# Attention and a gated MLP on one core: blocks of four slots as two or three visits with a written order, and tanh behind the scores

## The chip, the cores and the metric

One core of one Trainium2 chip. The time is that of one execution of the program on the device, in microseconds; all times below are in microseconds unless marked otherwise. The kernel before took 1624.26 in the median of three runs (1623.45 to 1624.9).

## The reference

The input x is 2048 tokens by 512 features. It is normalised (layernorm without gain), then goes through two branches: attention with 32 heads of 16 features, and an MLP of 512 to 1792 to 512 with a squared ReLU. The attention output is multiplied by silu of the MLP output and added to x.

```python
qkv = x @ wqkv                                     # 32 heads of 16
scores = einsum("bhqd,bhkd->bhqk", q, k) * 16 ** -0.5
s = softmax(scores) @ v  ->  @ wo
h = xn @ w1 + b1; r = where(h > 0, h, 0); out = (r * r) @ w2 + b2
return x + s * silu(out)
```

All of it is float32. The kernel keeps that precision by splitting operands into a high and a low part and running three matmuls for each product; attention scores carry the parts in extra rows of 64-row operands.

## The kernel before

**Slots and units.** Attention is cut into 32 units (a group of four heads and 512 queries), and each unit into 16 slots of 128 keys: 512 slots in all. A slot st has four **scores** (`exp_mm`, matmul on line 1225: 64 rows, 512 columns; then an exponential on ACT, line 1231, into a tile `pt` or `ex`) and, two slots later, one **PV** step (`pv_mm`, line 382): four column tiles of 128 rows by 32 columns, accumulated in the bank `po`. At the end of a unit `evac` copies `po` on ACT and starts a chain that divides by the row sums.

**Maxima.** The softmax needs the maximum of each row before the unit's first score. It is made ahead by `max_mm` (line 306: the same product once more; then a reduce on DVE, line 314): 64 maxima for each unit, 2048 in all. When a unit's maxima are complete, `max_end` notes it, and `shift_due` calls `shift` (lines 337 to 359): four short DVE instructions, and DMAs on SP that write the result into rows of the unit's query tiles.

**Dense work.** The MLP and the output product are run in between by a generator, `dense`. From slot 60 on most of it comes in blocks of four slots: 12 dense units (D) for each of the two **row tiles** of TensorE (partitions 0 to 63 and 64 to 127, the *lanes* 0 and 1). A D is one matmul of 512 columns (second MLP product and output product) or two of 256 (`first_pair`, first MLP product), on line 240 or 790. The two lanes add into one PSUM bank `pd_t`; the second lane's first matmul is made to wait for an instruction (`last_use`) that shows that the first lane is done. At the end of the block `post` empties the bank on ACT (two ReLUs, or a copy). Between the blocks stand stretches of four plain slots (`slot`, line 1356) with six D each.

**Banks.** Scores go through three PSUM banks (`se`), maxima through three others (`pm_t`), `pd_t` and `po` have one each. So the fourth score waits for the first one's exponential, and the fourth maximum for the first one's reduce.

**Who sets the order.** PE, ACT, DVE, POOL and SP run in the order in which the Python code records their instructions; no scheduler moves them. `long_slots` (line 1405) writes the order of a block: two halves h, each with the D of lane h. A half is either one **visit** of 14 steps per lane (all 12 D and two scores on lane h; six scores and seven maxima on the other) and then two PV steps in one group, or a visit of ten steps and one of four, each with one PV step behind it; that has eight maxima. `seven(st)` chooses the double form where the maxima are far enough ahead (`ahead_m`), always for two halves in a row: the second of a block and the first of the next. `visit` writes a column of the two strings at a time: the other lane's instruction, then its own.

**The gate.** After the second MLP product of 128 tokens, `gate` (line 579) is run three slots later, by `begin` at the start of a slot: tanh on ACT (line 581), two POOL instructions, and a DMA to `g_d`, which the output blocks read much later.

Of the kernel before, what the change touches and what calls it, by code (L numbers as in the profile page):

```python
# [18 lines left out]
D = 512  # L19
# [9 lines left out]
NCK = S // CW  # L29
# [4 lines left out]
EVAC = (1, 5, 6, 8, 12, 15)  # L34
EVAC_LAST = (1, 4, 5, 6, 8, 10)
EPS = 1e-5
LEAD_AT = (
    (3, 8, 12, 17, 22, 26, 31, 36, 40, 45, 48),
    (1, 6, 12, 15, 20, 24, 29, 33, 38, 42, 47),
# [4 lines left out]
def kernel(  # L44
# [54 lines left out]
    with ExitStack() as ph:  # L99
# [268 lines left out]
                    waiting.append((16 * u - 9, back))  # L368

        in_loop = []  # L370

        def shift_rows(u, p, i):
                    nc.sync.dma_start(
# [69 lines left out]
        def mlp_tasks(mp):  # L443
# [119 lines left out]
            def second(c, tt):  # L563
                hT = state["hT"]
                ps = pd.tile([P, D], F32, name="pd_t")
                u = up.tile([P, D], F32, name="u")
                th = rs[tt].rearrange("p a b -> p (a b)")
                ts_ = slice(tt * P, (tt + 1) * P)

                if c == 0 and tt == 0:  # L570
                    for k in range(5, FO):
                        later(k - 4, lambda k=k: load_w2(k, 2))

                def post():
                    nc.scalar.activation(u, ps, AF.Copy)  # L575
                    nc.gpsimd.tensor_tensor(u, u, b2_t, op=ALU.add)  # L576
                    later(3, gate)

                def gate():

                    nc.scalar.activation(th, u, AF.Tanh, scale=0.5)
                    nc.gpsimd.tensor_scalar(th, th, 0.5, 0.5, op0=ALU.mult, op1=ALU.add)
                    nc.gpsimd.tensor_tensor(u, u, th, op=ALU.mult)
                    t0 = c * CW + tt * P
                    later(4, lambda: nc.sync.dma_start(g_d[t0 : t0 + P, :], u))

                mms = terms3(ps, [
                    (lambda a, q, fo=fo: hT[q, a, fo, ts_], lambda b, q, fo=fo: w2t[q, b, fo])
                    for fo in range(FO)
                ])  # L590
                if c == 0:
                    yield from halves(mms, (6,) * 7, post, 1)
                    return
                if c == NCK - 1 and tt:

                    for i, task in enumerate(halves(mms, (6,) * 7, post, 1)):
                        if i == 4:
                            gone_pt.extend(rot["ex"])
                            free_pt[:] = [t for t in free_pt if all(t is not x for x in gone_pt)]
                        yield task  # L600
                    return

                if tt:
                    yield from halves(mms[:6], (6,), None, 1)
                    mms = mms[6:]
                for k in range(0, 36, 12):
# [626 lines left out]
        pts = {}  # L1233
# [95 lines left out]
        pos = {}  # L1329

        def pv_step(st, pts):
            u, kb = divmod(st, 16)
            if kb == 0:
                pos[0] = pv.tile([P, 512], F32, name="po")
            pv_mm(pos[0], u // 4, kb, pts)
            free_pt.extend(t for _, t in sorted(pts.items()) if all(t is not x for x in gone_pt))
            if kb == NT - 1:
                if u < NU - 2:
                    evac(pos[0], u)
                elif u == NU - 2:  # L1340
                    unit_inner(pos[0])
                else:
                    unit_final(pos[0])
# [61 lines left out]
        def long_slots(st0, units, post, wide=False):  # L1405
# [5 lines left out]
            def s(lane):  # L1411
                kb, j = todo[lane].pop(0)
                return exp_mm(kb, j, pts[kb], False)

            def visit(h, mine, theirs, h_first=False):
                own, other, follow = units[h], 1 - h, True
                for i, ops in enumerate(zip(mine, theirs)):
                    for lane in (h, other) if h_first else (other, h):
                        o = ops[0] if lane == h else ops[1]
                        if o == "D":  # L1420
                            own.pop(0)()
                        elif o == "m":
# [8 lines left out]
            wrap = [post] if post is not None else []  # L1431
            for h in range(2):
                st = st0 + 2 * h
                if st > st0:
                    begin(st)
                n = len(units[h])
                if wide:
                    for i, o in enumerate("sDsDDsDDDs"):
                        for lane in range(2):
                            if o == "s":  # L1440
                                s(lane)
                            else:
                                units[lane].pop(0)()
                    if wrap and not units[0]:
                        wrap.pop()()
                    begin(st + 1)
                    shift_due()
                    for kb in (st - 2, st - 1):
                        pv_step(kb, pts.pop(kb))
                elif n == 12 and seven(st):  # L1450
                    visit(h, "s" + "D" * n + "s", ".mmsmssmsmssmm")
# [122 lines left out]
```

## Time and profile before

| | before |
|---|---|
| median of three runs | 1624.26 (1623.45 to 1624.9) |
| the profiled execution | 1623.24 |
| its span, first to last instruction | 1621.4 |
| mean granted TensorE clock | 0.999 |
| PE busy | 1607.4 (99% of the span) |
| DVE busy | 1339.5 (83%) |
| ACT busy | 1184.9 (73%) |
| POOL busy | 526.4 (32%) |
| DMA traffic | 201.43 MB, mean 124 GB/s |

The page first gives each engine's busy time, then the chain of work that ended last, then groups of equal instructions with their number, the mean duration of one and the idle time ahead of them. Rows of the timeline begin with the start in us from the span's start and the duration of the row; a row with x7 merges seven instructions. In rows of PEld (weight loads) and the other engines, what stands in brackets is the idle time before and what ended it. `64*128` is a matmul on 64 rows and 128 columns of the array, `128*32` one on 128 rows and 32 columns. A row of the windows gives, for a stretch, its length, then busy time and number of instructions of PE, PEld, DVE, ACT and POOL, the granted clock, the DMA share and GB/s.

### The profile page before, as it was taken

The page shows a single profiled execution, that of the slowest core. Times are in us where ns is not written, and L with a number is a line of the kernel's source. Part 1 is how long each engine was busy: PE and PEld are TensorE (multiplying, and loading weights), DVE is VectorE, ACT ScalarE, POOL GpSimd, SP SyncE. Part 2 cuts the span into 40 slices and gives each one's busy share as a digit, 9 for nine tenths or more (in the row PEclk, how much of TensorE's full clock was granted, in tenths as well). Part 3 has the DMA queues.
Part 4 walks back from the last instruction along what each step waited for, and adds up shares of the span by engine and source line. Part 5 has one row for each costly group of instructions (what it writes and reads, how often), then busy time and mean ns, then how long its engine had stood idle before and what let it go on. Part 6 is the DMA issues. An engine that isn't in the chain of part 4 may idle for free.

```text
span 1621.4 us, 35371 instructions
## 1 busy us (share of the span) xinstructions
PE 1607.4 (99%) x13639; PEld 963.5 (59%) x13639; DVE 1339.5 (83%) x2327; ACT 1184.9 (73%) x2345; POOL 526.4 (32%) x549
## 2 busy tenths in 40 slices
PE   8999999999999999999999999999999999999998
PEld 6888665556556655665566556645665565554455
DVE  6499888888887888888888888888888888888833
ACT  6311777778777877777777778877877777777785
POOL 6635568223213320331132113311331133213334
PEclk9999999999999999999999999999999999999999
DMA  8895645334233631442342513333432342416443
GB/s 300 236 291 183 217 143 173 112 91 139 60 92 96 152 96 57 118 124 60 84 131 88 126 55 118 104 98 80 134 102 65 104 133 65 104 50 171 124 156 137
DMA packets 150464, 201.43 MB, mean 124 GB/s; under 512 B 50008, under 2 KB 67416, under 8 KB 148760
## 3 DMA queue, kind: packets, MB, share of 16 engines
q1 hardware_dynamic: 150296, 199.17, 41.9%
q8 instruction: 108, 1.77, 0.5%
q14 instruction: 60, 0.49, 0.1%
HBM read 144.84 MB, written 53.99 MB: 123 GB/s over the span
## 4 chain that ended last, share of the span: by engine, by line
PE 99%; DVE 0%; DMA 0%; ACT 0%; issue 0%; SPq 0%; DVEq 0%; ACTq 0%
PE po L382 31%; PE pd_t L240 18%; PE pm_t L306 17%; PE se L1225 15%; PE pd_t L208 6%; PE se L988 3%; PE se L1027 3%; PE pd_t L790 2%; PE po L1027 1%; PE pd_t L1027 1%; PE pm_t L1086 0%; PE pm_t L1225 0%; DMA xt<-in_A_x_dram 0%; PE pm_t L824 0%; PE se L872 0%; DVE mx L314 0%
## 5 line engine op out<-in xcount | busy, mean ns | idle before, releaser
L314 DVE TENSOR_REDUCE mx<-pm_t 128x1 f32<-128x512 f32 x2048 | 1266.2, 683 | 205.0 <-PE pm_t L306 111.9
L1231 ACT ACTIVATE pt<-se 128x512 f32<-128x512 f32 x1731 | 923.3, 613 | 217.9 <-PE se L1225 157.0
L306 PE MATMUL pm_t<-ka,qm 64*128 64x512 f32 x2048 | 790.0, 416 | 0.9 <-DVE mx L314 0.6
L1225 PE MATMUL se<-qe,ka 64*128 64x512 f32 x2009 | 728.4, 411 | 0.0
L382 PE MATMUL po<-pt,v 128*32 128x512 f32 x3540 | 527.9, 603 | 0.0
L306 PEld LDWEIGHTS pm_t<-ka,qm 64*128 64x128 f32 x2048 | 359.6, 184 | 219.8 <-DVE mx L314 199.5
L1225 PEld LDWEIGHTS se<-qe,ka 64*128 64x128 f32 x2009 | 349.8, 184 | 92.4 <-ACT pt L1231 63.9
L240 PEld LDWEIGHTS pd_t<-xc,w1s 64*128 64x128 f32 x2352 | 295.2, 187 | 53.0 <-issue 51.1
L240 PE MATMUL pd_t<-xc,w1s 64*128 64x256 f32 x2352 | 323.2, 286 | 0.0
L240 PE MATMUL pd_t<-w2t,hT 64*128 64x512 f32 x936 | 253.0, 406 | 0.0
L382 PE MATMUL po<-ex,v 128*32 128x512 f32 x556 | 233.9, 603 | 0.0
L1231 ACT ACTIVATE ex<-se 128x512 f32<-128x512 f32 x278 | 166.7, 614 | 49.9 <-PE se L1225 33.3
L240 PEld LDWEIGHTS pd_t<-w2t,hT 64*128 64x128 f32 x936 | 160.0, 184 | 50.5 <-issue 41.1
L382 PEld LDWEIGHTS po<-pt,v 128*32 128x32 f32 x3540 | 87.4, 108 | 150.1 <-issue 136.5
L557 POOL TENSOR_TENSOR r<-r 128x512 f32<-128x512 f32 x49 | 51.0, 1041 | 322.3 <-ACT r L554 322.3
L576 POOL TENSOR_TENSOR u<-u,b_t 128x512 f32<-128x512 f32 x16 | 20.6, 1289 | 361.3 <-ACT u L575 334.7
L208 PE MATMUL pd_t<-w2t,hT 64*128 64x512 f32 x408 | 106.0, 392 | 0.0
L208 PEld LDWEIGHTS pd_t<-w2t,hT 64*128 64x128 f32 x408 | 72.5, 184 | 10.3 <-DVE mx L314 0.7
L420 POOL TENSOR_TENSOR ot<-ot,hl 128x512 f32<-128x512 f32 x31 | 39.9, 1287 | 117.0 <-DMA hl<-r_d 86.7
L790 PE MATMUL pd_t<-wot,oc 64*128 64x512 f32 x267 | 76.1, 404 | 0.0
L84 POOL TENSOR_TENSOR hT<-r,hT 128x512 fp32r<-128x512 f32 x56 | 72.4, 1292 | 4.7
L554 ACT ACTIVATE r<-pd_t,b_t 128x256 f32<-128x256 f32 x98 | 42.2, 496 | 28.7 <-PE pd_t L240 28.7
(137 smaller groups left out, 1204.2 us busy)
## 6 DMA issues: line engine op xcount, KB each, us to landing
w1s<-w_d SPq DMA_DIRECT2D x196, 256.0 KB
xn_d<-xT SPq DMA_DIRECT2D x8, 1024.0 KB
qm<-q_d SPq DMA_DIRECT2D x128, 64.0 KB
qe<-q_d SPq DMA_DIRECT2D x128, 64.0 KB
ka<-k_d SPq DMA_DIRECT2D x32, 256.0 KB
hl<-r_d SPq DMA_DIRECT2D x31, 256.0 KB
k_d<-hl SPq DMA_DIRECT2D x30, 256.0 KB
q_d<-hl SPq DMA_DIRECT2D x15, 512.0 KB
```

Source lines behind the costliest of these rows:

```text
L84: (lo or nc.gpsimd).tensor_tensor(dst[1], raw, dst[0].bitcast(F32), op=ALU.subtract)
L208: mm = nc.tensor.matmul(out_, lh(r), rh(r), start=first_ and lane == 0, stop=last_ and lane == 1, skip_group_check=True,)
L240: mm = nc.tensor.matmul(out_, lh(r), rh(r), start=first_ and lane == 0, stop=last_ and lane == 1, skip_group_check=True,)
L306: nc.tensor.matmul(ps, qms[u][p][64 * j : 64 * j + 64, qb * P : (qb + 1) * P], kas[qd, p][64 * j : 64 * j + 64, kc * 512 : (kc + 1) * 512] ...
L314: return nc.vector.tensor_reduce(mxs[u][:, c, kc : kc + 1], ps, axis=AX.X, op=ALU.max)
L382: nc.tensor.matmul(po[32 * j : 32 * j + 32, :], vs[qd][:, (4 * kb + j) * VW : (4 * kb + j) * VW + 32], pts[j], start=(kb == 0), stop=(kb = ...
L557: nc.gpsimd.tensor_tensor(r, r, r, op=ALU.mult)
L790: inst = nc.tensor.matmul(ps[lane], oc[r, a, n, ts_], wot[r, b, n], start=m == 0 and (lane == 0 or wide), stop=m == kos and (lane == 1 or ...
L988: nc.tensor.matmul(out_, lh(slice(0, P)), rh(slice(0, P)), start=first_, stop=last_)
L1027: inst = nc.tensor.matmul(out_, lh(r), rh(r), start=first_ and lane == lane0, stop=last_ and lane != lane0, skip_group_check=True,)
L1225: nc.tensor.matmul(se, kas[qd, j // 2][b : b + 64, kb * P : (kb + 1) * P], qes[u][j // 2][b : b + 64, :], start=True, stop=True,)
L1231: return nc.scalar.activation(pts[j], se, AF.Exp, scale=0.25)
```

## The change

Blocks with 12 D on each lane take a new path in `long_slots`. It chooses one of four pairs of texts. Each text is a visit, written as pairs of letter and lane: `s` a score, `m` a maximum, `D` a dense unit. `TWO_TWO` and `TWO_TWO_END` have two visits of 27 (12 D, 8 s, 7 m each) and two double PV groups. `ONE_TWO_ONE` and `TWO_ONE_ONE` have three visits of 26, 24 and 6 (all 12 D of lane 0 with 7 s and 7 m; all 12 of lane 1 with 6 and 6; 3 and 3) and PV groups of one, two and one, or of two, one and one. The first pair is taken where the maxima are far enough ahead, the forms with END and the one that begins with two at the first block of a unit. A unit's `shift` is called with no slack ahead of a double group and with two slots of slack ahead of a single one.

Of the 88 blocks with MLP work, the written order now has 34 of two double groups, 39 of one, two, one and 15 of two, one, one (before: 9 with two double groups, 48 with one, 31 with four single ones). Two blocks of the output product take the new path as well. PV groups of the whole program go from 432 (352 single, 80 double) to 375 (238 and 137). The number of each kind of matmul is the same.

`gate` no longer runs its instructions itself (but for the last column of tokens): it puts them on a list, and `pv_step` runs the list, so that they stand ahead of the next PV step and behind the scores of the visit.

The core of the diff:

```diff
+TWO_TWO = (
+    "s1m0s1D0D0m1s1D0D0m1s1D0m1D0D0s1D0m1s1D0D0s1D0D0m1s1m0",
+    "s0m1m0D1D1s0m0D1s0D1D1m0s0D1D1D1s0D1s0m0D1D1s0m0D1m1s0",
+)
...
+ONE_TWO_ONE = (
+    "m1D0D0s1m1D0s1D0m1D0s1D0m1D0D0s1D0s1D0m1D0m1D0s1s0m1",
+    "m0D1s0D1s0D1D1m0D1s0m0D1m0D1D1s0s0D1m0D1D1s0D1m0",
+    "m0s1m0s1m1s0",
+)
...
+        behind = []
+
+        def run_behind():
+            while behind:
+                behind.pop(0)()
...
                 def gate():
-
+                    if c < NCK - 1:
+                        behind.append(gate_ops)
+                    else:
+                        gate_ops()
+
+                def gate_ops():
                     nc.scalar.activation(th, u, AF.Tanh, scale=0.5)
...
         def pv_step(st, pts):
+            run_behind()
             u, kb = divmod(st, 16)
...
+            if not wide and len(units[0]) == len(units[1]) == 12:
+                ends = st0 % 16 == 0
+                kept = 0 if late else max(0, 450 - st0) // 16 * 2
+                if ahead_m(sum(done_m) + 14 - kept, st0 + 4):
+                    visits, sizes = TWO_TWO_END if ends else TWO_TWO, (2, 2)
+                elif ends:
+                    visits, sizes = TWO_ONE_ONE, (2, 1, 1)
+                else:
+                    visits, sizes = ONE_TWO_ONE, (1, 2, 1)
+                at = st0
+                for text, size in zip(visits, sizes):
...
+                        if use is not None and behind_d[lane]:
+                            last_use[0], behind_d[lane] = use, False
+                    if size == 2:
+                        begin(at + 1)
+                    max_end()
+                    shift_due(0 if size == 2 or st0 >= 440 else 2)
+                    for kb in range(at - 2, at - 2 + size):
+                        pv_step(kb, pts.pop(kb))
+                    at += size
```

Three places show what moves. The first is on PE, in the block of slots 260 to 263, where its first PV steps (258 and 259) stand. Before, with a group of its own for each, and a visit of four steps between them; `pd_t` is dense work, `pm_t` a maximum, `se` a score, `po` the PV bank:

```order
L1225 MATMUL se_13303<-qe0_757,ka0_202 128x512
L240 MATMUL pd_t_13119<-w2t_2514,hT_11857 128x512
L382 MATMUL po_13236<-pt13_1263,v0_1478 32x512
L382 MATMUL po_13236<-pt3_1253,v0_1478 32x512
L382 MATMUL po_13236<-ex1_1271,v0_1478 32x512
L382 MATMUL po_13236<-pt5_1255,v0_1478 32x512
L240 MATMUL pd_t_13119<-w2t_2514,hT_11857 128x512
L306 MATMUL pm_t_13317<-ka0_202,qm0_199 128x512
```

After, behind one visit of 14 steps that ends with two scores and two maxima:

```order
L324 MATMUL pm_t_13315<-ka0_202,qm0_199 128x512
L1253 MATMUL se_13318<-qe1_758,ka1_203 128x512
L324 MATMUL pm_t_13321<-ka0_202,qm0_199 128x512
L405 MATMUL po_13238<-pt11_1261,v0_1478 32x512
L405 MATMUL po_13238<-pt10_1260,v0_1478 32x512
L405 MATMUL po_13238<-ex0_1270,v0_1478 32x512
L405 MATMUL po_13238<-ex2_1272,v0_1478 32x512
L405 MATMUL po_13238<-pt6_1256,v0_1478 32x512
L405 MATMUL po_13238<-pt9_1259,v0_1478 32x512
L405 MATMUL po_13238<-pt4_1254,v0_1478 32x512
L405 MATMUL po_13238<-pt2_1252,v0_1478 32x512
L1253 MATMUL se_13350<-qe0_757,ka0_202 128x512
```

The visit of four steps is gone here, and PV steps 258 and 259 are one group. The second place is the end of the first visit of the next block, slots 264 to 267, one of the form one, two, one. After, on PE:

```order
L324 MATMUL pm_t_13462<-ka0_202,qm0_199 128x512
L258 MATMUL pd_t_13119<-w2t_2514,hT_11857 128x512
L324 MATMUL pm_t_13466<-ka1_203,qm1_200 128x512
L258 MATMUL pd_t_13119<-w2t_2514,hT_11857 128x512
L1253 MATMUL se_13470<-qe1_758,ka1_203 128x512
L1253 MATMUL se_13473<-qe0_757,ka0_202 128x512
L324 MATMUL pm_t_13476<-ka1_203,qm1_200 128x512
L405 MATMUL po_13238<-ex2_1272,v0_1478 32x512
```

Before, the same PV step 262 stood in a double group, behind a visit of 14 steps:

```order
L306 MATMUL pm_t_13471<-ka1_203,qm1_200 128x512
L240 MATMUL pd_t_13119<-w2t_2514,hT_11857 128x512
L306 MATMUL pm_t_13475<-ka1_203,qm1_200 128x512
L1225 MATMUL se_13478<-qe1_758,ka1_203 128x512
L382 MATMUL po_13236<-ex1_1271,v0_1478 32x512
L382 MATMUL po_13236<-ex2_1272,v0_1478 32x512
```

Both have seven maxima; the last of them is now the last matmul of 13 steps, where it was the last but one of 14. The third place is on ACT: tanh (`r<-u`) among the exponentials (`pt<-se`, `ex<-se`) in one of the first MLP blocks of a column of tokens. Before and after:

```order
L1231 ACTIVATE ex1_1271<-se_14232 128x512
L1231 ACTIVATE pt10_1260<-se_14235 128x512
L1231 ACTIVATE pt4_1254<-se_14238 128x512
L581 ACTIVATE r1_2507<-u_13639 128x512
L1231 ACTIVATE pt8_1258<-se_14256 128x512
```
```order
L1259 ACTIVATE ex0_1270<-se_14222 128x512
L1259 ACTIVATE pt6_1256<-se_14225 128x512
L609 ACTIVATE r1_2507<-u_13639 128x512
L1259 ACTIVATE pt12_1262<-se_14246 128x512
```

Before, it is recorded when a slot begins, ahead of that slot's exponentials; now it is recorded behind a visit's last exponential and ahead of its PV step.

More of the change, by code (lines that the diff above doesn't have):

```diff
@@ L36 @@
 EPS = 1e-5
+TWO_TWO = (
+    "s1m0s1D0D0m1s1D0D0m1s1D0m1D0D0s1D0m1s1D0D0s1D0D0m1s1m0",
+    "s0m1m0D1D1s0m0D1s0D1D1m0s0D1D1D1s0D1s0m0D1D1s0m0D1m1s0",
+)
+TWO_TWO_END = (
+    "s1m0s1D0D0m1D0m1D0s1D0s1D0D0m1D0s1D0s1m1D0D0s1m1D0m0s1",
+    "m1s0D1s0m0D1m0D1s0D1D1s0m0D1D1s0D1D1s0D1m0D1s0m0D1m1s0",
+)
[3 more added lines that the diff above has]
+    "m0s1m0s1m1s0",
+)
+TWO_ONE_ONE = (
+    "m1D0s1D0m1D0D0s1D0m1s1D0m1D0s1D0D0s1D0m1m1D0D0s1s1m0",
+    "m0D1D1s0D1s0m0D1D1s0m0D1m0D1s0D1s0D1m0D1s0D1D1m0",
+    "s0m1s0m1s1m0",
+)
 LEAD_AT = (
@@ L1431, in long_slots @@
             wrap = [post] if post is not None else []
+            if not wide and len(units[0]) == len(units[1]) == 12:
[9 more added lines that the diff above has]
+                for text, size in zip(visits, sizes):
+                    if at > st0:
+                        begin(at)
+                    behind_d = [False, False]
+                    for k in range(0, len(text), 2):
+                        lane, use = int(text[k + 1]), None
+                        if text[k] == "D":
+                            units[lane].pop(0)()
+                            if not units[lane]:
+                                behind_d[lane] = True
+                                if lane and wrap:
+                                    wrap.pop()()
+                        elif text[k] == "s":
+                            use = s(lane)
+                        else:
+                            use = max_mm(lane)
+                        if use is not None and behind_d[lane]:
[7 more added lines that the diff above has]
+                    at += size
+                if post is not None:
+                    last_use[0] = None
+                assert not todo[0] and not todo[1] and not units[0] and not units[1]
+                return
             for h in range(2):
@@ L1450, in long_slots @@
                 elif n == 12 and seven(st):
-                    visit(h, "s" + "D" * n + "s", ".mmsmssmsmssmm")
+                    visit(h, "s" + "D" * n + "s", "msmsmsmsmsms.m", True)
                     begin(st + 1)
```

## The prediction

> **What bounds the kernel now.** I read the page's busy times first, then the chain of work that ended last, then the groups.
>
> ```profile
> PE 1607.4 (99%) x13639; PEld 963.5 (59%) x13639; DVE 1339.5 (83%) x2327; ACT 1184.9 (73%) x2345; POOL 526.4 (32%) x549
> ...
> PE 99%; DVE 0%; DMA 0%; ACT 0%; issue 0%; SPq 0%; DVEq 0%; ACTq 0%
> ...
> L314 DVE TENSOR_REDUCE mx<-pm_t 128x1 f32<-128x512 f32 x2048 | 1266.2, 683 | 205.0 <-PE pm_t L306 111.9
> L1231 ACT ACTIVATE pt<-se 128x512 f32<-128x512 f32 x1731 | 923.3, 613 | 217.9 <-PE se L1225 157.0
> ```
>
> PE is the chain, but a busy PE is not a PE at its pace: the question is how far apart its matmuls start. So the next view is PE's timeline, over a block of four slots with groups of one, one and two (512-column dense work). I call the matmuls between two PV groups a visit, and one 512-column matmul of a row tile a step.
>
> ```profile
> 903.82 0.49 PE L306 MATMUL pm_t<-ka,qm 64*128 64x512 f32 x1
> ...
> 904.16 0.39 PE L1225 MATMUL se<-qe,ka 64*128 64x512 f32 x1
> ...
> 906.03 0.39 PE L1225 MATMUL se<-qe,ka 64*128 64x512 f32 x1
> ...
> 906.36 0.62 PE L382 MATMUL po<-pt,v 128*32 128x512 f32 x2
> ...
> 907.36 0.49 PE L240 MATMUL pd_t<-w2t,hT 64*128 64x512 f32 x1
> ...
> 908.48 1.06 PE L382 MATMUL po<-pt,v 128*32 128x512 f32 x8
> 909.47 0.49 PE L1225 MATMUL se<-qe,ka 64*128 64x512 f32 x1
> ...
> 913.04 1.49 PE L382 MATMUL po<-pt,v 128*32 128x512 f32 x11
> ...
> 914.89 0.50 PE L1225 MATMUL se<-qe,ka 64*128 64x512 f32 x1
> ...
> 918.50 0.62 PE L382 MATMUL po<-ex,v 128*32 128x512 f32 x2
> ```
>
> In the visit of ten steps the first step takes 0.34 (903.82 to 904.16), the next eight 1.87, so 0.234 each, and the last 0.33 (906.03 to 906.36). A visit that waits for nothing thus lasts 0.20 + 0.234 per step: 2.54 for ten, 1.14 for four (here 1.12). A single PV group holds PE for 1.00 (906.36 to 907.36), a double one for 1.85 (913.04 to 914.89). So one group fewer is worth 2 x 1.00 - 1.85 = 0.15 and a start of 0.20, together 0.34 (unrounded).
>
> The visits before double groups are another thing: 909.47 to 913.04 is 3.57 and 914.89 to 918.50 is 3.61, where 14 steps free of waits would be 3.48. DVE, ACT and the weight loads say why.
>
> ```profile
> 915.46 4.28 DVE L314 TENSOR_REDUCE mx<-pm_t 128x1 f32<-128x512 f32 x7 [0.43 <-PE se L1225]
> ```
> ```profile
> 915.43 4.07 ACT L1231 ACTIVATE pt<-se 128x512 f32<-128x512 f32 x8 [1.39 <-PE se L1225]
> ```
> ```profile
> 917.58 0.18 PEld L1225 LDWEIGHTS se<-qe,ka 64*128 64x128 f32 x1 [0.30 <-ACT pt L1231]
> ...
> 918.00 0.18 PEld L306 LDWEIGHTS pm_t<-ka,qm 64*128 64x128 f32 x1
> 918.08 0.18 PEld L1225 LDWEIGHTS se<-qe,ka 64*128 64x128 f32 x1
> ```
>
> The first reduce starts 0.57 after the visit; the seven stand (4.28 - 0.68) / 6 = 0.60 apart. With three banks the seventh maximum waits for the fourth reduce, which starts at 2.37 and ends at 3.05; its weights are loaded at 918.00, 3.11 after the start. The last score is loaded at 918.08, behind eight exponentials (4.07 - 0.61) / 7 = 0.49 apart, and PV follows 0.42 later. **So a visit with seven maxima cannot reach its PV before 3.11 + 0.42 = 3.53, however few steps it has.** That limit decides this change. With 256-column dense work, two matmuls to a step, a 14-step visit is no shorter or longer:
>
> ```profile
> 559.07 0.50 PE L1225 MATMUL se<-qe,ka 64*128 64x512 f32 x1
> ...
> 562.68 0.62 PE L382 MATMUL po<-pt,v 128*32 128x512 f32 x2
> ```
>
> 3.61 again, so I reckon both widths alike.
>
> **The change, part by part.** The dense blocks lie between 342 and 1401 us, with six stretches of four plain slots among them.
>
> ```profile
> 342.00:1401.00 1059.00, 1058.99 (x9388) 617.69 (x9390) 906.15 (x1550) 828.53 (x1653) 268.31 (x264) 1.00 0.36 100
> 926.02:937.51 11.49, 11.49 (x92) 6.04 (x88) 10.11 (x17) 9.51 (x19) 4.02 (x4) 1.00 0.40 112
> ```
>
> 1059.0 - 6 x 11.49 = 990.1 us for 88 blocks before. The order of PE's instructions gives their groups: before, 9 blocks with two double groups, 48 with one, 31 with none, 286 groups; after, 34 blocks with two double ones and 54 with three groups, 230. The output blocks lose one group more and gain two visits with seven maxima; I set those at nothing. The maxima add up to 2048 in the same block as before, so no work goes elsewhere, and a block stays at 28 steps.
>
> - *Two double groups, 34 blocks.* Both visits keep 14 steps and seven maxima; one maximum and one score stand at the very end. The second score now stands one step in, not two, so ACT starts its second exponential without a hole and the last score can load a little before the 3.19 of now. Between the 3.53 of DVE and the 3.61 of now I take 3.56. A block: 2 x (3.56 + 1.85) = 10.82.
> - *Three groups, 54 blocks.* The visit of 13 steps would last 3.24 freely, but has seven maxima: 3.53, a loss of 0.29. The visit of 12 has six; its third maximum stands at the sixth step, is reduced from about 1.87 to 2.55, and the sixth loads at 2.61, so PV at 3.03 against 3.01 freely: 3.02. The visit of three: 0.90; its three reduces take 1.89, as in the row below, 0.5 after its start, and end at 2.4, where the next visit's first reduce begins at 1.90 + 0.57 = 2.47: clear, barely. A block: 3.53 + 1.00 + 3.02 + 1.85 + 0.90 + 1.00 = 11.30.
>
> ```profile
> 907.92 1.89 DVE L314 TENSOR_REDUCE mx<-pm_t 128x1 f32<-128x512 f32 x3 [0.48 <-PE pm_t L306]
> ```
>
> - *The end of a unit's maxima.* Its four short DVE instructions were put before single groups too, where the first reduce of the next visit had to follow them:
>
> ```profile
> 631.78 0.50 PE L306 MATMUL pm_t<-ka,qm 64*128 64x512 f32 x1
> ```
> ```profile
> 632.03 0.21 DVE L339 TENSOR_REDUCE sh<-mx 128x16 f32<-128x64 f32 x1
> ...
> 632.62 0.21 DVE L347 STREAM_TRANSPOSE sq<-sh 128x32 f32<-128x32 f32 x1
> 632.76 3.04 DVE L314 TENSOR_REDUCE mx<-pm_t 128x1 f32<-128x512 f32 x5
> ```
> The visit from 631.78 has its first reduce at 0.98 instead of 0.57. Now every block has a double group, and its 1.85 covers the four: nothing. Without that cover it is 0.4 each time. Their DMAs on SP follow one and three slots later, as now, with slots of 2.7 us to spare.
> - *tanh.* Before, it stood ahead of a visit's exponentials:
>
> ```profile
> 503.68 0.50 PE L1225 MATMUL se<-qe,ka 64*128 64x512 f32 x1
> ...
> 504.01 0.64 ACT L581 ACTIVATE r<-u 128x512 f32<-128x512 f32 x1
> ...
> 504.54 0.61 ACT L1231 ACTIVATE pt<-se 128x512 f32<-128x512 f32 x1
> ```
> ```profile
> POOL r L582 <- ACT r L581: 68.9, 16, 6.2
> ```
> The first exponential is 0.86 into that visit, not 0.54: 0.3 lost. Behind the visit's last score it runs while PV does, at no cost; if PV were single and short it would again cost the 0.3. The two POOL instructions after it come later by a visit; POOL waits for it 16 times and is busy 268 of 1059 us, and the store is not read until the output blocks.
>
> Sum: 34 x 10.82 + 54 x 11.30 = 978.1, against 990.1: -12.0. The other way round: 56 groups x 0.34 = -19, of which waits take back +7. I leave +1.2 for what the blocks above leave out (copies of the output on ACT at unit ends, the first dense block): **-10.8 us**. The profiled execution took 1623.24 (span 1621.4), so 1612.4; the median of the runs shown is 1.0 higher: **1613**.
>
> Bounds: with visits of 14 at 3.53 (-2.0), of 12 at 3.01 (-0.5) and nothing left out (-1.2): 1610. With 14 steps at the 3.61 of now (+3.4), 13 at 3.61 too (+4.3), 12 late by 0.1 (+5.4), and 3 for tanh and the short instructions uncovered: 1630.
>
> **The rivals.**
>
> *Waits eat it.* The hand-over limits all visits as they do now: the upper bounds above, or half of them: 1621 to 1630, about 1624. For it: the 0.08 that DVE has to spare after the visit of three, and the first dense matmul of the second row tile, which follows an exponential of the visit before. Against: the free visits of the trace keep their 0.234 to the hundredth.
>
> *Order between the row tiles: slower.* The new order has two dense units of one tile in a row, then one matmul of the other. With 256 columns a unit is two matmuls, and if starts keep the written order, the other tile starts half a step (0.117) late after each pair. 18 blocks with ten pairs, 25 with five, 6 with six: 341 x 0.117 = 40 us, so 1653; it decides once a quarter of that is real. The rows speak against it. In a four-step visit, where line 1467 writes the unit ahead of the maximum, and in a 14-step one, where line 1451 has a unit's two matmuls ahead of a score, the trace has:
>
> ```profile
> 501.56 0.38 PE L240 MATMUL pd_t<-xc,w1s 64*128 64x256 f32 x1
> ...
> 501.57 0.50 PE L306 MATMUL pm_t<-ka,qm 64*128 64x512 f32 x1
> ...
> 501.78 0.40 PE L240 MATMUL pd_t<-xc,w1s 64*128 64x256 f32 x2
> ```
> ```profile
> 559.41 0.18 PEld L1225 LDWEIGHTS se<-qe,ka 64*128 64x128 f32 x1
> 559.52 0.30 PEld L240 LDWEIGHTS pd_t<-xc,w1s 64*128 64x128 f32 x2
> ```
> The maximum starts 0.21 before the second half of the unit written ahead of it, and the score's weights are loaded ahead of both halves; more than that the new order doesn't ask for. The Trainium skill, TensorE: Matmul & The Clock Gate, Part 3 (The mechanism), says that matmuls start and end strictly in program order and only weight loads are pulled ahead; by it the sum would be 1653. The rows at 501 differ from it, so it gets little weight.
>
> *No DVE limit.* Visits at their free lengths: 54 x 0.29 + 68 x 0.08 = 21 us less, 1592. The rows at 918 speak against it.
>
> **How the numbers follow.** Forecast 0.66 (1608 to 1620), waits 0.22 (0.03 faster, 0.14 the same, 0.05 slower), order 0.07, no limit 0.05. Range 1606 to 1624: it leaves out the order, the missing limit and part of the waits. Two in a thousand (3.2 us) is about what a measurement tells from no change. Faster 0.66 + 0.03 + 0.05 = 0.74, same 0.14, slower 0.05 + 0.07 = 0.12.
>
> **What would show it.** Right: PV of a 13-step visit 3.53 after its start with its last maximum loaded at 3.11; 12 steps near 3.02; 14 near 3.56; tanh with no exponential behind it waiting. Wrong: 13 steps over 3.7 (then nothing is left), 256-column visits longer than 512-column ones by several tenths, or a first reduce later than 0.6.

## The result, and the profile after

The changed kernel takes **1620.55** (median of 12 runs, 1619.64 to 1621.82); the kernel before, run beside it, 1624.17 (12 runs, 1623.45 to 1626.01). The ratio is 0.9978, 95% interval 0.9970 to 0.9986. That is 3.6 faster, where 10.8 was forecast: the side is right and the time lies in the range, but the size is a third.

The profiled execution took 1621.74 (span 1620.0). The page of the kernel after, busy times, chain and groups; the lines of the code have moved: maxima are on 324 and their reduces on 332, scores on 1253 and exponentials on 1259, dense work on 226 and 258, PV on 405.

```profile
PE 1605.6 (99%) x13639; PEld 990.3 (61%) x13639; DVE 1340.7 (83%) x2327; ACT 1185.1 (73%) x2345; POOL 525.1 (32%) x549
...
PE 98%; DMA 1%; SPq 0%; DVE 0%; ACT 0%; issue 0%; DVEq 0%
...
L332 DVE TENSOR_REDUCE mx<-pm_t 128x1 f32<-128x512 f32 x2048 | 1267.2, 683 | 202.7 <-PE pm_t L324 118.9
L1259 ACT ACTIVATE pt<-se 128x512 f32<-128x512 f32 x1738 | 924.6, 611 | 246.6 <-PE se L1253 150.5
...
L324 PEld LDWEIGHTS pm_t<-ka,qm 64*128 64x128 f32 x2048 | 366.9, 184 | 255.8 <-DVE mx L332 227.2
...
L1253 PEld LDWEIGHTS se<-qe,ka 64*128 64x128 f32 x2009 | 359.5, 184 | 109.6 <-ACT pt L1259 68.9
```

The picture is that of before, with one row to look at: weight loads of maxima now wait 227.2 in all for a reduce. The same rows of before had 199.5 for maxima and 63.9 for scores, so by the page the added wait stands at the maxima (27.7) and hardly at the scores (5.0); the runs below show that the exponentials hold the visits as well:

```profile
L306 PEld LDWEIGHTS pm_t<-ka,qm 64*128 64x128 f32 x2048 | 359.6, 184 | 219.8 <-DVE mx L314 199.5
...
L1225 PEld LDWEIGHTS se<-qe,ka 64*128 64x128 f32 x2009 | 349.8, 184 | 92.4 <-ACT pt L1231 63.9
```

For the dense blocks, the windows from the first block's first matmul to the end of the last, less the six plain stretches between (the sums of their windows). Before:

```profile
341.86:1400.40 1058.54, 1058.53 (x9387) 617.31 (x9384) 905.83 (x1550) 828.18 (x1652) 268.31 (x264) 1.00 0.36 100
...
sum 69.54, PE 69.54 PEld 36.52 DVE 62.27 ACT 57.22 POOL 10.48; mean PE 11.59 PEld 6.09 DVE 10.38 ACT 9.54 POOL 1.75
```

After:

```profile
343.68:1398.70 1055.02, 1055.02 (x9385) 641.94 (x9381) 905.04 (x1548) 828.43 (x1652) 267.54 (x264) 1.00 0.37 100
...
sum 69.43, PE 69.43 PEld 36.50 DVE 62.42 ACT 54.04 POOL 7.73; mean PE 11.57 PEld 6.08 DVE 10.40 ACT 9.01 POOL 1.29
```

The 88 blocks took 989.0 before and 985.6 after: -3.4, where -12.0 was worked out. The plain stretches are the same. In this execution the first block starts 1.8 later than in that of before, which is why the spans differ by only 1.4; the medians differ by 3.6. The 1.8 is scatter: six kernels below, which differ from one of the two only in the blocks or in where tanh stands, start their first block anywhere from 341.7 to 344.0. So what is missing of the forecast is missing inside the blocks. One of them, of the form one, two, one, on PE's timeline (start, duration, engine, line, operation):

```profile
1016.02 0.49 PE L324 MATMUL pm_t<-ka,qm 64*128 64x512 f32 x1
...
1019.52 0.62 PE L405 MATMUL po<-pt,v 128*32 128x512 f32 x2
...
1020.52 0.50 PE L324 MATMUL pm_t<-ka,qm 64*128 64x512 f32 x1
...
1023.64 0.62 PE L405 MATMUL po<-ex,v 128*32 128x512 f32 x1
...
1025.49 0.50 PE L324 MATMUL pm_t<-ka,qm 64*128 64x512 f32 x1
...
1026.38 0.63 PE L405 MATMUL po<-pt,v 128*32 128x512 f32 x3
...
1027.38 0.49 PE L324 MATMUL pm_t<-ka,qm 64*128 64x512 f32 x1
```

The visit of 13 steps takes 3.50 (forecast 3.53), that of 12 takes 3.12 (forecast 3.02), that of three 0.89 (0.90); groups 1.00, 1.85, 1.00. The block: 11.36 instead of 11.30. In the 13 steps the last maximum's weights are loaded 3.07 after the start, where 3.11 was forecast:

```profile
1019.09 0.18 PEld L324 LDWEIGHTS pm_t<-ka,qm 64*128 64x128 f32 x1
```

And a block of two double groups, its first visit from 1038.72 and its second from 1044.15:

```profile
1038.72 0.49 PE L1253 MATMUL se<-qe,ka 64*128 64x512 f32 x1
...
1042.29 0.62 PE L405 MATMUL po<-ex,v 128*32 128x512 f32 x1
...
1044.15 0.50 PE L1253 MATMUL se<-qe,ka 64*128 64x512 f32 x1
...
1047.79 0.62 PE L405 MATMUL po<-pt,v 128*32 128x512 f32 x2
```

3.57 and 3.64, where 3.56 was forecast for both. Over all visits of the dense blocks in the trace, from the first matmul to PV, in the forecast's terms:

| | number | forecast | measured, mean | difference in all |
|---|---|---|---|---|
| 14 steps | 68 | 3.56 | 3.621 | +4.1 |
| 13 steps | 54 | 3.53 | 3.498 | -1.7 |
| 12 steps | 54 | 3.02 | 3.119 | +5.3 |
| 3 steps | 54 | 0.90 | 0.895 | -0.3 |
| double PV group | 122 | 1.85 | 1.854 | +0.5 |
| single PV group | 108 | 1.00 | 0.996 | -0.4 |
| sum of the blocks | 88 | 978.1 | 985.6 | +7.5 |

The 14 steps are 3.58 in the first visit of a block and 3.66 in the second (3.646 in 25 blocks, 3.706 in the nine that begin a unit).

### The profile page after: what moved, and what is told of

It reads as the page before. It is cut to its first block, busy times and chain, and to the rows that moved or that the text cites. A ratio compares the mean times of both kernels' runs of the same rounds, so it can differ in the third digit from the quotient of the medians.

```text
span 1620.0 us, 35384 instructions
## 1 busy us (share of the span) xinstructions
PE 1605.6 (99%) x13639; PEld 990.3 (61%) x13639; DVE 1340.7 (83%) x2327; ACT 1185.1 (73%) x2345; POOL 525.1 (32%) x549
## 4 chain that ended last, share of the span: by engine, by line
PE 98%; DMA 1%; SPq 0%; DVE 0%; ACT 0%; issue 0%; DVEq 0%
PE po L405 30%; PE pm_t L324 19%; PE se L1253 17%; PE pd_t L258 15%; PE pd_t L226 6%; PE se L1055 3%; PE pd_t L818 2%; PE se L1016 2%; PE po L1055 2%; PE pd_t L1055 1%; PE pm_t L1114 0%; DMA ka<-k_d 0%; PE pm_t L1253 0%; DMA xc<-xn_d 0%; DMA k_d<-hl 0%; PE pm_t L852 0%
## 5 line engine op out<-in xcount | busy, mean ns | idle before, releaser
L324 PE MATMUL pm_t<-ka,qm 64*128 64x512 f32 x2048 | 778.3, 419 | 1.4 <-DVE mx L332 0.6
L1253 PE MATMUL se<-qe,ka 64*128 64x512 f32 x2009 | 748.0, 421 | 0.0
L324 PEld LDWEIGHTS pm_t<-ka,qm 64*128 64x128 f32 x2048 | 366.9, 184 | 255.8 <-DVE mx L332 227.2
L405 PE MATMUL po<-pt,v 128*32 128x512 f32 x3554 | 516.4, 601 | 0.0
L1253 PEld LDWEIGHTS se<-qe,ka 64*128 64x128 f32 x2009 | 359.5, 184 | 109.6 <-ACT pt L1259 68.9
L258 PE MATMUL pd_t<-xc,w1s 64*128 64x256 f32 x2352 | 305.4, 283 | 0.0
L258 PE MATMUL pd_t<-w2t,hT 64*128 64x512 f32 x936 | 239.1, 400 | 0.0
L405 PE MATMUL po<-ex,v 128*32 128x512 f32 x542 | 223.8, 601 | 0.0
L405 PEld LDWEIGHTS po<-pt,v 128*32 128x32 f32 x3554 | 93.2, 108 | 161.4 <-issue 150.2
L226 PE MATMUL pd_t<-w2t,hT 64*128 64x512 f32 x408 | 105.9, 392 | 0.0
L405 PEld LDWEIGHTS po<-ex,v 128*32 128x32 f32 x542 | 37.0, 108 | 26.3 <-issue 24.5
```

Source lines behind the costliest of these rows:

```text
L226: mm = nc.tensor.matmul(out_, lh(r), rh(r), start=first_ and lane == 0, stop=last_ and lane == 1, skip_group_check=True,)
L258: mm = nc.tensor.matmul(out_, lh(r), rh(r), start=first_ and lane == 0, stop=last_ and lane == 1, skip_group_check=True,)
L324: nc.tensor.matmul(ps, qms[u][p][64 * j : 64 * j + 64, qb * P : (qb + 1) * P], kas[qd, p][64 * j : 64 * j + 64, kc * 512 : (kc + 1) * 512] ...
L405: nc.tensor.matmul(po[32 * j : 32 * j + 32, :], vs[qd][:, (4 * kb + j) * VW : (4 * kb + j) * VW + 32], pts[j], start=(kb == 0), stop=(kb = ...
L1253: nc.tensor.matmul(se, kas[qd, j // 2][b : b + 64, kb * P : (kb + 1) * P], qes[u][j // 2][b : b + 64, :], start=True, stop=True,)
```

## The experiments

**What is a PV group worth, and who takes it back?** A **hand-over** is here the time from the start of the reduce or exponential that empties a bank to the load of the weights that fill it again: 0.73 and 0.65 in the rows below. The theory formed on the trace after: a group fewer is worth what was reckoned, and the visits are held by *two* hand-overs, reduces with three banks and exponentials with three banks. Rivals: only the maxima hold them; or something in the written order itself does. Eight kernels make a table: before and after, each whole, with reduces over half of their columns, with exponentials over half of theirs, with both. What they leave out is half of the maxima and of the exponentials; all matmuls stay. The kernels with short exponentials also fill the tiles `pt` with ones on POOL when these are made, so that the half that no exponential writes holds a number. The two edits:

```diff
-                mxs[u][:, c, kc : kc + 1], ps, axis=AX.X, op=ALU.max
+                mxs[u][:, c, kc : kc + 1], ps[:, :256], axis=AX.X, op=ALU.max
...
-            return nc.scalar.activation(pts[j], se, AF.Exp, scale=0.25)
+            return nc.scalar.activation(pts[j][:, :256], se[:, :256], AF.Exp, scale=0.25)
```

Reduces cut, in the kernel before:

> The kernel before with each maximum's reduce over 256 of the 512 columns, so half the keys are left out of the maxima; all matmuls stay. The theory of the waits says that in the old order the 14-step visits are held by scores and exponentials as much as by the reduces, and the ten-step ones hardly by either: 14 steps go from 3.61 to about 3.58, in all 2 to 4 us less than before (1621). The rival, that neither DVE nor the banks hold anything and the lengths come from TensorE itself: no change.

The same in the kernel after:

> The changed kernel with each maximum's reduce over 256 of the 512 columns, so half the keys are left out of the maxima; all matmuls and their order stay. The theory of the waits: the seventh maximum no longer waits for the fourth reduce, visits of 13 steps go from 3.50 to about 3.32 (then held by the seventh score), of 12 from 3.12 to 3.06, of 14 from 3.61 to 3.58, in all 13 us less than the changed kernel (1607), so that the distance to the kernel before with the same cut reaches 13 us where it is 3.6 now. The rival, that a new order with two dense units of one row tile in a row costs TensorE time: 13 steps stay at 3.50 and the distance stays under 5 us.

Exponentials cut, in the kernel before:

> The kernel before, with each exponential of a score over 256 of its 512 columns (half of the exponentials is left out), the maxima whole. It completes a table of four pairs: before and after, each whole, with short reduces, with short exponentials, with both. So far after lies 3.6 below before when both are whole, 9.1 with short reduces, 18.7 with both. Theory (maxima and exponentials hold the visits of after together, and either alone leaves most of the waits): with short exponentials alone the distance is 7 to 10, so this kernel takes 1617 to 1620. Rival (the exponentials alone account for what is missing): 12 to 15, so 1622 to 1625.

The same in the kernel after:

> The kernel after, with each exponential of a score over 256 of its 512 columns (the other half of the probability tile keeps an earlier value), so that ACT needs about 0.2 less for each. The maxima are as in the kernel after. My theory: the 12- and 14-step visits are held by the hand-over between exponentials and scores (two scores in a row wait for an exponential of 0.49), the 13-step visits by the maxima. Then 12 steps go from 3.12 to 3.03-3.05, 14 steps from 3.58-3.70 to 3.53-3.56 (the maxima's limit), 13 steps stay at 3.50, and the time falls by about 8, to 1612. Rival (the maxima hold all visits): all lengths stay and the time stays within 2 of 1620.5.

Both cut, in the kernel before:

> The kernel before, with each reduce of a maximum and each exponential over 256 of 512 columns (half of the maxima and half of the exponentials are left out). Both hand-overs are then shorter by some 0.2 to 0.3. Theory: 14-step visits 3.50 instead of 3.61, few others change: about 1614, 10 below the kernel before. This is the base for the same cut in the kernel after.

Both in the kernel after:

> The kernel after with the same cut as in both_before: reduces of maxima and exponentials over 256 of 512 columns. If the 56 PV groups fewer are worth 0.32 to 0.34 each and only the two hand-overs take it back, then the distance to both_before is 56 x 0.32 = 18, and the visits have their free lengths: 13 steps 3.25, 12 steps 3.02, 14 steps 3.49. Rival (something in the written order itself, such as two dense units of one row tile in a row, takes the rest): the distance stays under 12 and the visits stay 0.1 or more above the free lengths.

Measured, medians with the interval of the ratio to the whole kernel before (12 runs of each whole kernel, four of each other one):

| | before | after | after is faster by |
|---|---|---|---|
| whole | 1624.17 | 1620.55 (0.9970 to 0.9986) | 3.6 |
| short reduces | 1616.49 (0.9940 to 0.9967) | 1607.37 (0.9886 to 0.9913) | 9.1 |
| short exponentials | 1616.98 (0.9942 to 0.9972) | 1610.02 (0.9900 to 0.9930) | 7.0 |
| both | 1602.49 (0.9856 to 0.9883) | 1583.80 (0.9743 to 0.9770) | 18.7 |

Four runs leave such a difference open by about 3. The traces say the same more closely: from the first dense block's start to the last one's end, after is shorter by 3.5, 9.3, 7.8 and 18.6. With both hand-overs shortened, 56 groups fewer are worth 18.7, or 0.334 each: the 0.34 of the prediction. With both in place 15.1 of it is lost. Relief of one alone brings back only 5.5 or 3.4, less together than both at once, since a visit ends when the later of the two allows it. The rival that the written order costs something falls with the 18.7; the rival that only the maxima count falls with 7.0 and with the visits.

Not all that was expected came. The kernel before gained more from the cuts than forecast (1616.49 where 1621 was expected, 1602.49 where 1614 was): with short reduces its 14 steps stayed at 3.62, its ten steps went from 2.588 to 2.552 in the mean, and about half of the gain lies outside the dense blocks. In the kernel after, short reduces left the 12 steps at 3.12 where 3.06 was expected, and the distance came to 9.1 and not to 13.

The 13-step and the 12-step visit after it, with short reduces, on PE:

```profile
1006.94 0.49 PE L324 MATMUL pm_t<-ka,qm 64*128 64x512 f32 x1
...
1010.31 0.62 PE L405 MATMUL po<-pt,v 128*32 128x512 f32 x2
...
1011.30 0.50 PE L324 MATMUL pm_t<-ka,qm 64*128 64x512 f32 x1
...
1014.42 0.62 PE L405 MATMUL po<-ex,v 128*32 128x512 f32 x1
```

With short exponentials:

```profile
1008.67 0.50 PE L324 MATMUL pm_t<-ka,qm 64*128 64x512 f32 x1
...
1012.18 0.62 PE L405 MATMUL po<-pt,v 128*32 128x512 f32 x2
...
1013.17 0.50 PE L324 MATMUL pm_t<-ka,qm 64*128 64x512 f32 x1
...
1016.24 0.62 PE L405 MATMUL po<-ex,v 128*32 128x512 f32 x1
```

Short reduces take the 13 steps from 3.50 to 3.37 and leave the 12 at 3.12; short exponentials leave the 13 at 3.51 and take the 12 to 3.07. Over all visits of the kernel after and its cut forms, means:

| steps | whole | short reduces | short exponentials | both |
|---|---|---|---|---|
| 14 | 3.621 | 3.598 | 3.534 | 3.478 |
| 13 | 3.498 | 3.358 | 3.499 | 3.256 |
| 12 | 3.119 | 3.117 | 3.044 | 3.022 |

So the 13 steps are held by the maxima, and the 12 and 14 by the exponentials first. With both short, 12 steps take 3.02 in the mean, as the prediction had it, but by chance: the 31 with 256-column dense work take 3.065 and the 23 with 512 columns 2.963, where it reckoned both widths alike.

**Why 12 steps take 3.12.** In the visit from 1020.52 the loads of scores and maxima at its end, then ACT:

```profile
1022.49 0.18 PEld L1253 LDWEIGHTS se<-qe,ka 64*128 64x128 f32 x1
...
1022.97 0.18 PEld L1253 LDWEIGHTS se<-qe,ka 64*128 64x128 f32 x1
...
1023.15 0.18 PEld L324 LDWEIGHTS pm_t<-ka,qm 64*128 64x128 f32 x1
```
```profile
1021.35 2.07 ACT L1259 ACTIVATE pt<-se 128x512 f32<-128x512 f32 x4 [0.99 <-PE se L1253]
```

The first score stands behind a maximum, so the first exponential starts at 0.83 and the second one 0.49 later, at 1.32. The fifth score, the second of two in a row at the eighth and ninth step (7 and 8 when counted from nought, as the text below has it), is loaded at 1.97, 0.65 after that start, and all that stands behind it on its row tile follows late. Theory: the two scores in a row do it. So a text in which maximum and score take turns until the last steps:

```diff
-    "m0D1s0D1s0D1D1m0D1s0m0D1m0D1D1s0s0D1m0D1D1s0D1m0",
+    "m0D1s0D1m0D1s0D1m0D1s0D1m0D1s0D1m0D1s0D1s0D1m0D1",
...
-    "m0D1D1s0D1s0m0D1D1s0m0D1m0D1s0D1s0D1m0D1s0D1D1m0",
+    "m0D1s0D1m0D1s0D1m0D1s0D1m0D1s0D1m0D1s0D1s0D1m0D1",
```

> The kernel after, with only the text of the 12-step visit changed (54 visits, both forms with three groups): maximum and score of row tile 0 take turns strictly until the last three, so that the first two scores in a row stand at the end and not at steps 7 and 8. Theory (the exponentials' hand-over at the two scores in a row holds the visit at 3.12): 12 steps fall to 3.05-3.07, and the time by 2.5 to 3.5, to about 1617.5. Rival (the maxima hold it, or the alternation of the tiles): 3.10 to 3.13, and a time within 1 of the kernel after.

It took 1620.45 (0.9971 to 0.9989), the same as the kernel after. The forecast was a miss. The trace says how: in the 15 visits of the form two, one, one the 12 steps went from 3.10 to 3.06 as expected, but in the 39 of the form one, two, one they stayed at 3.13. Such a visit begins at 1018.58:

```profile
1021.04 0.18 PEld L1253 LDWEIGHTS se<-qe,ka 64*128 64x128 f32 x1
...
1021.15 0.19 PEld L324 LDWEIGHTS pm_t<-ka,qm 64*128 64x128 f32 x1
...
1021.71 0.11 PEld L405 LDWEIGHTS po<-ex,v 128*32 128x32 f32 x1
```
```profile
1019.41 2.07 ACT L1259 ACTIVATE pt<-se 128x512 f32<-128x512 f32 x4 [0.97 <-PE pd_t L258]
```

The sixth score is loaded at 2.46: the third exponential starts at 0.83 + 2 x 0.49 = 1.81, and 0.65 later its bank is free. In the kernel after it is loaded at 2.45 as well (1022.97). So the order in the middle is not what counts. The sixth score cannot load before 2.46 when the first exponential starts at 0.83, the sixth maximum cannot before the third reduce allows it at 0.54 + 2 x 0.60 + 0.73 = 2.47, and both stand on one row tile: from the load of the first of them to PV it takes 0.67 (1021.04 to 1021.71). That is 3.13. In the form two, one, one with this text the first exponential starts at 0.77, and the sixth score is loaded at 2.39 instead of 2.46 (medians).

The other side, a visit that begins with the score:

```diff
+    "s0D1m0D1s0D1m0D1s0D1m0D1s0D1m0D1s0D1m0D1s0D1m0D1",
```

> The kernel after, with the 12-step visits (54) beginning with a score, and maximum and score taking turns to the end. It tests the hand-over on the maxima's side. Theory: the first reduce starts at 0.83 instead of 0.54, the sixth maximum waits for the third reduce (0.83 + 2 x 0.60 + 0.73 = 2.76) and PV follows 0.42 later: 3.18 instead of 3.12, so the time rises by about 3, to 1623.5. Rival (the exponentials hold these visits in any order): the exponentials start 0.3 sooner, so 3.03 to 3.06 and a time of 1616 to 1617.5.

1622.41 (0.9982 to 1.0000), 12 steps 3.14 in all 54: longer than the 3.12 of the kernel after, as the hand-over of the maxima says, but by 0.02 for each visit and not by 0.06, since the first reduce starts at 0.77 and not at 0.83. Over 54 visits that is 1.1; the medians differ by 1.9, and their intervals overlap. In the visit from 1020.07 the reduces, the exponentials, and the last maximum's load with PV's first one:

```profile
1020.84 3.08 DVE L332 TENSOR_REDUCE mx<-pm_t 128x1 f32<-128x512 f32 x5 [0.45 <-PE pm_t L324]
```
```profile
1020.61 2.08 ACT L1259 ACTIVATE pt<-se 128x512 f32<-128x512 f32 x4 [0.68 <-PE pd_t L258]
```
```profile
1022.78 0.18 PEld L324 LDWEIGHTS pm_t<-ka,qm 64*128 64x128 f32 x1
...
1023.21 0.11 PEld L405 LDWEIGHTS po<-ex,v 128*32 128x32 f32 x1
```

The third reduce starts at 0.77 + 1.20 = 1.97, the maximum loads at 2.71 and PV follows 0.43 later. Whichever stands first, the other is a step late. The rival is out, since the exponentials here start at 0.54 and the visit is no shorter for it.

**Why 14 steps take 3.58 and 3.65.** The second text of `TWO_TWO` has two maxima ahead of its second score, the first text has one. The second was replaced by the first with its row tiles exchanged:

```diff
-    "s0m1m0D1D1s0m0D1s0D1D1m0s0D1D1D1s0D1s0m0D1D1s0m0D1m1s0",
+    "s0m1s0D1D1m0s0D1D1m0s0D1m0D1D1s0D1m0s0D1D1s0D1D1m0s0m1",
```

> The kernel after, with only the second text of the form with two double groups replaced by the first one with its row tiles exchanged (25 visits of 14 steps). In the kernel after the first text takes 3.58 and the second 3.65, because its second maximum stands ahead of its second score and a waiting maximum delays two scores. Theory: the order in the text is the cause, so the second visit falls to 3.575 and the time by 1.8, to about 1618.8. Rival (what stands before the visit, or the row tile, is the cause): it stays at 3.65 and the time within 0.5 of the kernel after.

1619.33 (0.9960 to 0.9982): 1.2 less than the kernel after, where 1.8 was expected, and the intervals overlap. The visits are clearer: 25 second visits went from 3.646 to 3.574, and those of the first text stayed. One, from 860.87 on:

```profile
860.87 0.50 PE L1253 MATMUL se<-qe,ka 64*128 64x512 f32 x1
...
864.43 0.62 PE L405 MATMUL po<-pt,v 128*32 128x512 f32 x2
```
```profile
864.01 0.18 PEld L1253 LDWEIGHTS se<-qe,ka 64*128 64x128 f32 x1
```
```profile
861.40 0.60 ACT L1259 ACTIVATE pt<-se 128x512 f32<-128x512 f32 x1 [1.41 <-PE pm_t L324]
861.89 0.59 ACT L1259 ACTIVATE ex<-se 128x512 f32<-128x512 f32 x1
862.37 2.56 ACT L1259 ACTIVATE pt<-se 128x512 f32<-128x512 f32 x5
```

The eighth score waits for the fifth exponential. That is the third of the last five shown, which start (2.56 - 0.60) / 4 = 0.49 apart: at 862.37 + 0.98 = 863.35, 2.48 into the visit. The load is at 864.01, 3.14, and PV 0.42 later: 3.56. This is the limit of a visit with eight scores, and it lies above the 3.53 of seven maxima.

**Both together, and the unit ends.** A kernel with that text, the same exchange in the form for a unit's end, and the alternating text for the form two, one, one alone:

> The kernel after with three texts changed: both second texts of the forms with two double groups are the first ones with exchanged row tiles, and the 12-step visit of the form two, one, one has the alternating text of the run alt12, which took it from 3.10 to 3.06. Expected: 25 visits less by 0.07, 9 by up to 0.13 (none, if the output copy on ACT at a unit's end holds these), 16 by 0.04: 2.4 to 3.6 less, so 1617 to 1618, below both kernels. Rival: the waits move on to the next visit and the time stays within 1 of 1620.5.

**1618.39** (0.9955 to 0.9980), 5.5 less than the kernel before that ran beside it (1623.85), where the kernel after was 3.6 less. Against the kernel after the intervals overlap, and the gain is read from the visits: 25 second visits take 3.574, and the 12 steps of the form two, one, one 3.06, which makes 2.4 in all. The nine second visits at a unit's start did not move (3.706 and 3.704), so their text is not what holds them. In the one from 536.32, ACT:

```profile
536.51 0.60 ACT L415 ACTIVATE ot<-po 128x512 f32<-128x512 f32 x1 [1.04 <-issue]
537.00 2.06 ACT L1259 ACTIVATE pt<-se 128x512 f32<-128x512 f32 x4
```

The copy of the output bank starts at 0.19, and the first exponential at 0.68 instead of 0.53: 0.15 later, about the difference to 3.57. All nine have the copy ahead of their first exponential, and no other second visit has; in the one from 626.55 it starts at 0.13, the first exponential at 0.63, and the visit takes 3.66 instead of 3.71. No kernel with that copy elsewhere was run, so this is read from the trace alone.

**tanh and the order apart.** The tanh behind the scores alone, in the kernel before:

> The kernel before, with the gate's tanh and POOL instructions put behind the scores of a visit and nothing else changed. In the trace of before, four visits into which a tanh falls last 3.90 instead of 3.61, and four more are 0.1 to 0.2 longer than their like. If those are the tanh's doing: 1.7 us less than before (1622.5), and the four visits at 3.61. If they come from something else at the same place (the first dense matmul waiting for the bank): within 0.5 us of before.

1622.81 (0.9983 to 1.0001): 1.3 less, with an interval that just includes no change. The visits show it: the four of 3.90 are gone (the longest is 3.64), and the 14-step visits with 256-column work went from 3.635 to 3.607. And the order alone, with tanh where it stood:

> The changed kernel with the tanh where it stood before, so the new order of the blocks alone. If the tanh is worth in the new order what it cost in the old: 1 to 2 us over the changed kernel (1622), with visits that are 0.3 longer where a tanh stands ahead of the exponentials. If the double groups cover it anyway: the same as the changed kernel (1620.5).

1621.18 (0.9974 to 0.9991), 0.6 above the kernel after, within its spread; the mean lengths of the visits are those of after to 0.002. In the new order moving tanh is worth nothing that these runs can tell.

## Why the prediction was right in kind and too large in size

- **The value of a group** was right: 0.34 was reckoned, 0.334 measured with the hand-overs shortened. The Trainium skill, TensorEngine Tiling (Array Packing), Key Properties, says that a change of the tiling mode drains TensorE. A group fewer takes two such changes away, and the 0.334 fits that; no run here shows how much of it is the drain.
- **13 steps** were right: bounded by seven maxima on three banks, 3.53 against 3.498. Short reduces shorten them (3.358), short exponentials do not (3.499).
- **12 steps: here it failed.** The prediction sized their maxima (the sixth loaded at 2.61, PV at 3.03) but not their scores, and took 3.02. They cost 3.12, +5.3 in all. Six scores on three banks, with the first exponential at 0.83, and the last score and last maximum on one row tile gave 3.06 to 3.14 in the three orders that were run. The bound by the maxima was sound: with short exponentials the last maximum of the form one, two, one is loaded at 2.63 and PV follows at 3.06 (medians). A smaller part of the miss is the width: with 256-column work these visits take 3.065 even with both hand-overs short, and "I reckon both widths alike" rested on 14-step visits, which waits held. The upper bound had this price ("12 late by 0.1 (+5.4)"); the value taken was the lower one.
- **14 steps: the other term that failed**, +4.1. The prediction took 3.56, "between the 3.53 of DVE and the 3.61 of now"; eight exponentials alone give 3.57. The first visit kept to it (3.58). The ground that the prediction gave, a second score one step in, does not hold for the second text of `TWO_TWO`, which begins `s0m1m0D1D1s0`: there a maximum stands between the first two scores of the row tile, and that text cost another 0.07. At a unit's end it is 0.13, with the copy ahead of the exponentials.
- **The base** was 1.1 too high (990.1 against 989.0), because one plain stretch of 11.49 stood for a mean of 11.59 and the window's ends were rounded. The +1.2 left for the rest, the copies at unit ends above all, is by the trace what nine copies cost (9 x 0.13), though no run takes it apart; in the table it is part of the 14 steps. The 1.8 ahead of the first block is scatter.
- **The rival *waits eat it*** described the result best, though its 1621 to 1630 begins just above the 1620.55. With 19 for the groups and +7 for waits, the prediction kept 12; the waits took 15. It named the first reduce and the first dense matmul as the places, and the runs put them at the exponentials of the 12- and 14-step visits.
- **Order between the row tiles** is out. With both hand-overs short, 14 steps of 256-column work last 3.536 in the new order, with units in pairs, and 3.535 in the old one, where units and the other tile take turns. The rule that starts keep the written order (the Trainium skill, TensorE: Matmul & The Clock Gate, Part 3, The mechanism) would have the first longer by 0.117 for each of its five pairs, some 0.6; these visits disagree with it.
- **No DVE limit** is out as well: 13 steps last 3.50 and fall when the reduces do.
- **The short instructions at the end of a unit's maxima and tanh** were covered, as forecast: in the trace after, wherever the four stand in the dense blocks, they end ahead of the next visit's first reduce, which starts at 0.57 or earlier.

## What to carry to other kernels

Where a stage hands its results over a few banks to two engines, work out the earliest end for each of them with the same formula (first start, plus one spacing for each result beyond the banks but the first, plus the hand-over, plus the tail: three spacings for seven maxima on three banks, four for eight scores), and take the later; a bound worked out for the busier engine says nothing of a visit in which the other has more to do or starts later. Where a sum is a large gain less a large loss, an error of 0.1 in a visit that occurs 54 times is half of the forecast, so each such visit needs the bounds of both engines. And to see what a saving is worth by itself, shorten what would hide it in both kernels: 18.7 appeared where the plain comparison shows 3.6.

## What the runs showed of the hardware

Dense work of 256 columns, two matmuls to a step, is a little slower than of 512, but the waits of the 14-step visits hide it. In the kernel after the 14-step visits are alike (3.622 and 3.619). With both hand-overs short they are 3.536 and 3.412, 0.009 for each step (12 steps 3.065 and 2.963), as in these two visits of that kernel, the first with 256 columns and the second with 512:

```profile
353.52 0.49 PE L1255 MATMUL se<-qe,ka 64*128 64x512 f32 x1
...
357.05 0.64 PE L405 MATMUL po<-pt,v 128*32 128x512 f32 x4
...
428.73 0.50 PE L1255 MATMUL se<-qe,ka 64*128 64x512 f32 x1
...
432.14 0.64 PE L405 MATMUL po<-pt,v 128*32 128x512 f32 x4
```

And halving the columns does not halve the engine's time: a reduce went from 0.683 to 0.422 and an exponential from 0.611 to 0.383.

```profile
L332 DVE TENSOR_REDUCE mx<-pm_t 128x1 f32<-128x256 f32 x2048 | 813.9, 422 | 620.4 <-PE pm_t L324 389.9
L1261 ACT ACTIVATE pt<-se 128x256 f32<-128x256 f32 x1738 | 620.1, 383 | 485.7 <-PE pm_t L324 151.9
```
